# Cross read, GLU and soft mixture of experts on one core: the order of the opening, of batches 0 and 1 and of the end, and TensorE's turns for the states' rows

## The chip, the cores and the metric

The kernel runs on one core of one Trainium2 chip. The metric is the device time of one execution in microseconds (us), the median of three runs. A core has five engines that run side by side, each through its own instructions in program order: TensorE (PE in the profile, its weight loads PEld), VectorE (DVE), ScalarE (ACT), GpSimd (POOL) and SyncE (SP), which here only issues DMA transfers. They wait for each other through semaphores.

## What is computed

8 batches, each with 512 rows and 32 states, 8 heads of 64. Attention in both directions gives 512 + 32 rows of 512 for each batch; all 4608 rows go through a gated linear unit with 1536 inner columns, and its output through a soft mixture of 8 experts with 4 slots each.

```python
scores = scale * x @ state.T;  a = softmax(scores, -1);   xread = a @ state     # 512 rows a batch
scores2 = scale * state @ x.T; a2 = softmax(scores2, -1); sread = a2 @ x        # 32 rows a batch
x = concat(xread, sread)                                   # 4608 rows of 512
xn = x / sqrt(mean(x * x) + 1e-6) * rms_g
h = silu(xn @ w_gate) * (xn @ w_val)                       # 1536 columns
y = h @ w_out
logits = y @ phi                                           # 32 slots
d = softmax(logits, over rows); slot_in = d.T @ y          # 32 slots of 512
for e in range(8): slot_out[e] = relu(slot_in[e] @ w1[e]) @ w2[e]
out = softmax(logits, over slots) @ slot_out
```

## The kernel before

Work goes in nine groups: batches 0 to 7, each 4 tiles of 128 rows, and group 8 (`sread_group`), the 8 x 32 states' rows as 2 tiles. The 1536 inner columns are three chunks `c` of 512. Nothing of y is stored: the read-out of `h` by `w_out` is folded into the logits (`wphi`, that is `w_out @ phi`) and into the slot sums (`slot_h`), which are carried from group to group with a running maximum.

A group and chunk goes like this, each step a short verb in the scripts below. `sw` multiplies a weight chunk with the batch's states on TensorE (8 records; its last argument `r` is the half of the array's rows, 0 or 1), ScalarE copies the product into `wp` (L585), `ss` takes the rounding rest on VectorE (L590). `mg` and `mv` are the gate's and the value's matmul group for one tile, 6 records (12 in group 8), into one of three PSUM buffers of tag `mm`; `sl` is the silu on ScalarE (L624), which frees the gate's buffer; `h` is the product on VectorE (L632), which frees the value's. For the logits, `h` must be turned. In batches 0 and 1 TensorE turns it: `hT` is four 128x128 transposes (L116) and one copy from PSUM (L643, by its last argument on VectorE or ScalarE), and `lg` is then 8 records with 128 rows (`lg_mm128`). In groups 2 to 8 VectorE turns it in 32x32 blocks (`tp`, L660; `tt`, L675, one tile of group 8), and `lg` comes in halves, each 64 matmuls of 32x32 with a weight load for each (`lg_mm`). `p1`, `p2`, `pe`, `p3`, `ps` take the logits through their running softmax; `p1` (L704, L710) copies them out of PSUM, for the 32x32 form half on VectorE, half on ScalarE. `sh` is `slot_h`, the slot sums of one chunk.

Weights arrive as 64-bit words: `wl` loads a piece, `cb` begins it on ScalarE, each `ch` converts half on VectorE (L200, L204, L208) and ends with an add on GpSimd (L212). All of these stand in the opening, two per batch later. `rs` and `ri` are small reciprocals on VectorE. `warm n` are n filler matmuls of 128x128, `br` four, `table` a small exponential that makes ScalarE load its table. `pf` issues one 1 MB load of expert weights, `exp` opens a pool and issues four.

The order of every engine is the order in which the verbs are written: `EARLY` (the opening, batches 0 and 1, the start of 2), `BATCH` (a template for batches 2 to 5, `+0` this batch, `+1` the next), and `LATE` (batches 6, 7 and group 8), run by `follow` under a manual schedule. Behind the scripts stand the last logits' softmax (`post2`, with filler `keep_warm(6)` and `keep_warm(4)`), the slot sums of group 8 and the experts, whose weights come in 12 loads at the end as buffers become free.

Of the kernel before, what the change touches and what calls it, by code (L numbers as in the profile page):

```python
# [20 lines left out]
def kernel(  # L21
# [16 lines left out]
    nc = tc.nc  # L38
# [562 lines left out]
    HH, HT, LGP = {}, {}, {}  # L601
    xsg_t = {}
# [110 lines left out]
    def post2(g):
# [3 lines left out]
        for i in range(2 if g > 1 else 1):  # L717
            for t in range(n):
                o = ps[32 * t : 32 * t + 32, :P]
                if g > 1:  # L720
                    o = o.rearrange("p (b i m) -> p i b m", b=2, i=2)[:, i]
                mm(o, RH[0][:, i, :] if g > 1 else r32, Q[g, "lgs"][t])
# [128 lines left out]
    def wphi_sel():  # L851
# [14 lines left out]
    def wphi_spread(r):  # L866
# [9 lines left out]
        )  # L876

# [174 lines left out]
sw 0 1 1 0; sl 0 1 1; e2 1; warm 1; mg 1 0 3; ss 0 1 1 0; h 1 0 2; sl 1 0 3; ch; mv 1 0 3
sw 0 1 1 1; rs 1; b3 0; ss 0 1 1 1; h 1 0 3; ch; mg 0 1 2; b1 1 0; mg 0 1 3; wl; cb; sl 0 1 2; wl
mv 0 1 0; mv 0 1 1; h 0 1 0; cb; b1 1 1; ch; sl 0 1 3; mv 0 1 2; h 0 1 1; h 0 1 2; ch; mv 0 1 3
sw 0 2 0 0; h 0 1 3; xn 1; sw 0 2 0 1; sw 1 1 0 0; ss 0 2 0 0; ch; ss 1 1 0 0; ss 0 2 0 1; cb; ch
b2 1; sw 1 1 0 1; warm 1; ch; ch; cb; mg 0 2 3; mg 0 2 2; warm 3; sl 0 2 2; sw 0 2 1 0; ss 0 2 1 0
sw 0 2 1 1; mg 0 2 0; wl; sl 0 2 3; ss 0 2 1 1; mg 0 2 1; sl 0 2 0; ss 1 1 0 1; wl; b3 1; mv 0 2 0
h 0 2 0; sl 0 2 1; ch; hT 0 0 0 0; sw 1 1 1 0; mv 0 2 1; hT 0 0 1 0; cb; h 0 2 1; ch; hT 0 0 2 0; ch
cb; mv 0 2 2; mv 0 2 3; ss 1 1 1 0; wp 0 1; wp 0 0; wa 0 0; wa 0 1; warm 2; ch; mg 1 1 0; h 0 2 2
wq 0; sw 1 1 1 1; xt 2; ch; z 2; hT 0 0 3 0; sl 1 1 0; hT 0 1 0 0; mg 1 1 1; wp 1 0; ss 1 1 1 1  # L1060
h 0 2 3; mv 1 1 1; wl; mv 1 1 0; ch; wa 1 0; wl; h 1 1 0; sl 1 1 1; g 2; hT 0 2 0 0; wp 1 1; cb
lg 0 0; ch; a3 2 0; wa 1 1; hT 0 1 1 1; cb; hT 0 1 2 0; a3 2 1; cx 2 0; wq 1; hT 0 1 3 0; ch
mg 1 1 3; cx 2 1; sw 1 2 1 0; tr 2; h 1 1 1; hT 0 2 1 0; hT 1 0 0 0; wp 2 0; ch; tm 2; lg 0 1
mg 1 1 2; wa 2 0; run; ss 1 2 1 0; ts 2; mv 1 1 2; xt 3; sl 1 1 2; sl 1 1 3; ea 2; mv 1 1 3; h 1 1 2
wl; sw 1 2 0 0; hT 0 2 2 0; h 1 1 3; ch; hT 1 0 1 1; hT 0 2 3 1; ss 1 2 0 0; nc 2; sw 1 2 0 1
ss 1 2 0 1; sw 1 2 1 1; ss 1 2 1 1; wp 2 1; wa 2 1; mg 1 2 0; sm 2; wq 2; e2 2; mg 1 2 1; lg 0 2
nm 2 1; p1 0; bt 2; sl 1 2 0; sl 1 2 1; mv 1 2 1; p2 0; bc 2; rs 2; gram 2; pe 0; a3 3 0; bl 2
# [22 lines left out]
h +0 2 3; tp +0 2 1; a3 +2 1; cm +2; lg +0 1 0; tr +2; tm +2; z +2; lg +0 1 1; ts +2  # L1090
# [15 lines left out]
sl 7 0 1; tp 6 2 1; sl 7 0 0; ssum; lg 6 2 0; lg 6 2 1; mv 7 0 1; p1 6; mg 7 0 3; h 7 0 0; ssplit
h 7 0 1; tp 7 0 0; mg 7 0 2; p2 6; ss 7 1 0 1; sl 7 0 3; sl 7 0 2; pf 1; pe 6; mv 7 0 2; ss 7 1 0 0
# [343 lines left out]
```

## Time and profile before

| | us |
|---|---|
| three runs | 645.22, 647.32, 648.64 |
| median | 647.32 |
| the execution that was profiled | 648.35 |
| its span | 646.5 |
| TensorE busy | 615.6 |
| VectorE busy | 457.3 |
| ScalarE busy | 322.6 |
| GpSimd busy | 148.8 |

The profile is of one execution. Its span goes from the first to the last instruction that it records. An engine's busy time is what its instructions cover; a line such as L590 is a line of the kernel. Where an engine stood idle, the profile names what released it, or "issue" where it waited for nothing that the profile shows. The opening with batches 0 and 1 lasts to about 181 us, the four template batches to about 402, and the last main matmul of group 8 ends at 551.39.

### The profile page before, as it was taken

The numbers are of one execution on the slowest core, as the hardware profiler recorded it, in microseconds if no ns is written. First come the engines' busy times: TensorE is split into PE (matmuls) and PEld (weight loads), VectorE is DVE, ScalarE is ACT, GpSimd is POOL, SyncE is SP. The second block draws the span as 40 slices with busy tenths as digits, with TensorE's granted clock in tenths as the row PEclk, the third lists the DMA queues.
The fourth block names the chain that finished last, engine by engine and source line by source line (L and its number), as shares of the span: only waits on it lengthen the run. The fifth ranks groups of instructions, "written<-read, shape, count | busy, mean of one in ns | idle before, by whom it ended". The sixth has DMA issues, their size and how long they took to land.

```text
span 646.5 us, 15895 instructions
## 1 busy us (share of the span) xinstructions
PE 615.6 (95%) x6820; PEld 403.2 (62%) x6820; DVE 457.3 (71%) x902; ACT 322.6 (50%) x506; POOL 148.8 (23%) x183
## 2 busy tenths in 40 slices
PE   5999999999999999999999999999999999899982
PEld 3758666556466676667666675766566768753351
DVE  5988998887958786876877887679476666322152
ACT  4696685567485346346534733851452375100062
POOL 3354444532212021212203211312000000001530
PEclk9999999999999999999999999999999999779997
DMA  8924053530412023022102303200161275949968
GB/s 346 421 99 131 1 196 132 200 133 3 164 52 84 2 99 135 4 87 84 66 2 101 135 2 99 68 1 34 67 257 71 67 261 188 398 162 394 417 228 331
DMA packets 19990, 92.44 MB, mean 143 GB/s; under 512 B 2000, under 2 KB 3408, under 8 KB 12880
## 3 DMA queue, kind: packets, MB, share of 16 engines
q1 hardware_dynamic: 19632, 91.36, 37.5%
q8 instruction: 53, 0.87, 0.6%
q14 instruction: 17, 0.14, 0.1%
q10 hardware_dynamic: 288, 0.07, 0.0%
HBM read 79.37 MB, written 12.06 MB: 141 GB/s over the span
## 4 chain that ended last, share of the span: by engine, by line
PE 80%; DVE 8%; DMA 5%; issue 3%; ACT 3%; SPq 0%; DVEq 0%; ACTq 0%
PE mm L88 47%; PE misc L88 22%; PE lg L88 5%; PE misc L116 3%; DMA ew<-in_w_dram 3%; DVE wp L590 1%; DMA stT<-in_st_t_dram 1%; PE mm L111 1%; DMA out_dram<-ob 1%; DVE wo L208 1%; DVE w L208 1%; DVE w L204 1%; DVE wo L204 0%; DVE h L632 0%; DVE wo L200 0%
## 5 line engine op out<-in xcount | busy, mean ns | idle before, releaser
L88 PE MATMUL mm<-wp,A 128*128 128x512 f32 x1152 | 288.1, 399 | 1.8 <-DVE wp L590 1.4
L88 PEld LDWEIGHTS mm<-wp,A 128*128 128x128 f32 x1152 | 209.6, 188 | 80.1 <-issue 18.0
L585 ACT CAST wp<-misc 128x512 fp32r<-128x512 f32 x96 | 52.8, 590 | 135.5 <-PE misc L88 135.4
L624 ACT ACTIVATE sg<-mm,rinv 128x512 f32<-128x512 f32 x102 | 69.1, 691 | 60.7 <-PE mm L88 40.8
L632 DVE SCALAR_TENSOR_TENSOR h<-mm,rinv,sg 128x512 f32<-128x512 f32 x102 | 75.5, 743 | 26.7 <-PE mm L88 17.8
L590 DVE TENSOR_TENSOR wp<-misc,wp 128x512 fp32r<-128x512 f32 x96 | 63.8, 682 | 13.6 <-ACT wp L585 12.8
L88 PE MATMUL misc<-w,stTg 64*32 64x512 f32 x768 | 64.4, 601 | 0.0
L660 DVE STREAM_TRANSPOSE hT<-h 128x1024 f32<-128x1024 f32 x38 | 46.6, 1235 | 0.3
L88 PE MATMUL lg<-hT,wphi_x 32*32 32x128 f32 (+1 forms) x1344 | 41.4, 264 | 4.0 <-issue 3.8
L88 PEld LDWEIGHTS lg<-hT,wphi_x 32*32 32x32 f32 x1344 | 35.2, 104 | 14.4 <-issue 12.0
L88 PE MATMUL misc<-hT,wphi_x 32*32 32x128 f32 (+1 forms) x1344 | 41.9, 265 | 0.0
L212 POOL TENSOR_TENSOR wo<-wo,raw 128x512 int32<-128x512 int32 x18 | 23.6, 1310 | 70.1 <-ACT sg L624 26.6
L212 POOL TENSOR_TENSOR w<-w,raw 128x512 int32<-128x512 int32 x20 | 26.4, 1322 | 42.3 <-DVE w L208 22.8
L88 PEld LDWEIGHTS misc<-hT,wphi_x 32*32 32x32 f32 x1344 | 34.2, 104 | 2.3 <-issue 2.3
L88 PE MATMUL mm<-wh,xsg 128*128 128x512 f32 x96 | 30.9, 395 | 0.0
L624 ACT ACT_TABLE_LOAD x21 | 26.9, 1283 | 5.6 <-issue 4.7
L88 PE MATMUL misc<-h,ET 128*32 128x512 f32 x204 | 26.3, 599 | 0.8 <-DVE ET L777 0.8
L88 PEld LDWEIGHTS lg<-ident 128*128 128x128 f32 x156 | 20.9, 210 | 6.7 <-issue 5.0
L505 POOL TENSOR_TENSOR A<-aT,A 128x1024 fp32r<-128x1024 f32 x7 | 16.9, 2412 | 33.2 <-ACT A L501 26.9
L88 PE MATMUL lg<-ident 128*128 128x128 f32 x156 | 22.5, 298 | 1.4 <-POOL ident masks.py:199 1.4
L1191 POOL MEMSET sinE<- 128x512 f32 x2 | 1.0, 524 | 96.0 <-PE mm L88 96.0
L88 PEld LDWEIGHTS misc<-w,stTg 64*32 64x32 f32 x768 | 10.8, 105 | 18.6 <-issue 14.7
(246 smaller groups left out, 909.9 us busy)
## 6 DMA issues: line engine op xcount, KB each, us to landing
ew<-in_w_dram SPq DMA_DIRECT2D x25, 1024.0 KB, 7.4
xT<-in_x_t_dram SPq DMA_DIRECT2D x8, 1024.0 KB, 5.4
xn<-in_x_n_dram SPq DMA_DIRECT2D x8, 1024.0 KB, 6.0
ew_w<-in_w_dram SPq DMA_DIRECT2D x7, 1024.0 KB, 9.0
raw<-in_w_val_dram SPq DMA_DIRECT2D x6, 1024.0 KB, 10.5
raw<-in_w_out_dram SPq DMA_DIRECT2D x6, 1024.0 KB, 5.3
raw<-in_w_gate_dram SPq DMA_DIRECT2D x4, 1024.0 KB, 10.5
out_dram<-ob SPq DMA_DIRECT2D x4, 1024.0 KB, 5.9
```

The source lines that it names most:

```text
L88: nc.tensor.matmul(out=o, lhsT=lhsT, rhs=rhs, start=start, stop=stop)
L111: tc.keep_in_program_order(nc.tensor.matmul(out=ps[:, :P], lhsT=ident, rhs=ident, start=True, stop=True))
L116: nc.tensor.transpose(o, i, ident)
L204: nc.vector.tensor_scalar(out=a[:, h], in0=a[:, h], scalar1=3, scalar2=0x3FFFFFF8, op0=ALU.logical_shift_left, op1=ALU.bitwise_and,)
L208: nc.vector.scalar_tensor_tensor(out=a[:, h], in0=hi[:, h], scalar=-0x40000000, in1=a[:, h], op0=ALU.bitwise_and, op1=ALU.bitwise_or,)
L212: nc.gpsimd.tensor_tensor(out=a[:, h], in0=a[:, h], in1=rnd[:, h], op=ALU.add)
L505: nc.gpsimd.tensor_tensor(out=A[:, :, 1, :], in0=T[b, "aT"], in1=A[:, :, 0, :].bitcast(F32), op=ALU.subtract)
L585: nc.scalar.copy(t[:, r, 0, :], ps)
L590: nc.vector.tensor_tensor(out=t[:, r, 1, :], in0=T.pop(("sw", b, c, gv, r)), in1=t[:, r, 0, :].bitcast(F32), op=ALU.subtract,)
L624: nc.scalar.activation(out=sg, in_=ps, func=AF.Silu, scale=RINV[g][:, t : t + 1])
L632: nc.vector.scalar_tensor_tensor(out=HH[g, c][:, t, :], in0=ps, scalar=RINV[g][:, t : t + 1], in1=sg, op0=ALU.mult, op1=ALU.mult,)
L660: nc.vector.transpose(HT[g, c][:, 2 * j : 2 * j + 2, :].rearrange("p t f -> p (t f)"), HH[g, c][:, 2 * j : 2 * j + 2, :].rearrange("p t f ...
```

## The change

Group 8 now takes the form of batches 0 and 1. `by_pe` names the groups that TensorE turns; `lg_mm128`, `logits`, `post1` and `post2` ask it instead of `g < 2`, and take the width of the group, 256 columns. It needs `wphi` in its plain layout to the end, so GpSimd copies it once into the tile of the selector matrices behind `w4 3`.

```diff
+    by_pe = (0, 1, sread_group)
 def lg_mm128(g, c):
-        hT = HT.pop((g, c))
+        hT, n = HT.pop((g, c)), P * gsize(g)
+        w = WPHI4[1] if g > 1 else wphi
-                LGP[g][32 * q : 32 * q + 32, :], wphi[:, 4 * c + q, :], hT[:, q, :],
+                LGP[g][32 * q : 32 * q + 32, :n], w[:, 4 * c + q, :], hT[:, q, :n],
 def logits(g, c, half=1):
-        if g > 1:
+        if g not in by_pe:
 def post1(g):
-        if g < 2:
+        if g in by_pe:
 def post2(g):
-        for i in range(2 if g > 1 else 1):
+        for i in range(1 if g in by_pe else 2):
-                mm(o, RH[0][:, i, :] if g > 1 else r32, Q[g, "lgs"][t])
+                mm(o, r32 if g in by_pe else RH[0][:, i, :], Q[g, "lgs"][t])
 def wphi_spread(r):
+        if r == 3:
+            WPHI4.append(SEL[4])
+            nc.gpsimd.tensor_copy(SEL[4], wphi)
```

All three scripts are written anew. `EARLY` has the same verbs in another order, 82 filler matmuls for 78, and eight of the `hT` copies on VectorE for six. `BATCH` has the same verbs; TensorE's order in it is the same, VectorE's and ScalarE's are not. `LATE` has the same verbs but for group 8: `tp 8`, `tt 8`, the six halves `lg 8 c half` and `br; br` go, six `hT` and three `lg 8 c` come. `exp` stands later, behind `sw 7 2 1 1`. The last lines of `LATE`:

```diff
-table; sl 8 2 1; pf 1; h 8 2 0; tt 8 2 0; h 8 2 1; sh 7 2; pf 1; tt 8 2 1; br; br; lg 8 2 0
-lg 8 2 1; p1 8; pf 1
+mv 8 2 0; h 8 2 0; h 8 2 1; lg 8 1; hT 8 2 0 0; hT 8 2 1 0; sh 7 2; lg 8 2; table; p1 8; pf 1; pf 1
```

TensorE at the end of group 8, before: `hT_6311` and `hT_6440` are the turned chunks 1 and 2, `misc<-h_5822,ET` is `sh 7 2`, `misc<-ident` is `br; br`. The pair of `lg` and `misc` rows stands 16 times for each chunk.

```order
1124 L88 MATMUL lg_6170<-hT_6311,wphi_x_1751 32x64 x2
1125 L88 MATMUL misc<-hT_6311,wphi_x_1751 32x64 x2
1126 L88 MATMUL misc<-h_5822,ET 32x512 x4
1127 L88 MATMUL misc<-ident 128x128 x8
1128 L88 MATMUL lg_6170<-hT_6440,wphi_x_1751 32x64 x2
1129 L88 MATMUL misc<-hT_6440,wphi_x_1751 32x64 x2
```

The same place on TensorE now: L116 with `h_6339` are the turns of chunk 2, `misc<-lgs` is `p2`.

```order
1056 L88 MATMUL mm<-wh_6248,xsg_5421 128x512
1057 L88 MATMUL lg_6179<-hT_6275,wphi_x_1758 32x256 x4
1058 L116 MATMUL misc<-ident,h_6339 128x128 x8
1059 L88 MATMUL misc<-h_5822,ET 32x512 x4
1060 L88 MATMUL lg_6179<-hT_6351,wphi_x_1758 32x256 x4
1061 L88 MATMUL misc<-lgs,r_75 32x128 x2
1062 L111 MATMUL mm<-ident 128x128 x6
```

The 128 small matmuls and the filler behind the last main group are gone, and the turns of chunk 2 stand in front of `sh 7 2`.

TensorE in batch 6, before: the end of chunk 1's logits (`hT_5027`), which here follow the second half of chunk 0's directly; then the `sw` of batch 7 (`misc<-w,stTg`) and main matmuls.

```order
785 L88 MATMUL lg_5117<-hT_5027,wphi_x_1751 32x128 x2
786 L88 MATMUL misc<-hT_5027,wphi_x_1751 32x128 x2
787 L88 MATMUL misc<-w_105,stTg 32x512 x8
788 L88 MATMUL mm<-wp_4973,A_4216 128x512 x6
789 L88 MATMUL mm<-wp_4920,A_4216 128x512 x6
790 L88 MATMUL mm<-wp_4973,A_4216 128x512 x6
791 L88 MATMUL misc<-w_212,stTg 32x512 x8
792 L88 MATMUL mm<-wp_5282,A_4942 128x512 x12
```

The same work now: `hT_4874` is chunk 0, `hT_5037` chunk 1.

```order
745 L88 MATMUL lg_5110<-hT_4874,wphi_x_1758 32x128 x2
746 L88 MATMUL misc<-hT_4874,wphi_x_1758 32x128 x2
747 L88 MATMUL misc<-w_101,stTg 32x512 x8
748 L88 MATMUL mm<-wp_4975,A_4221 128x512 x6
749 L88 MATMUL mm<-wp_4890,A_4221 128x512 x6
750 L88 MATMUL misc<-w_198,stTg 32x512 x8
751 L88 MATMUL lg_5110<-hT_5037,wphi_x_1758 32x128 x2
752 L88 MATMUL misc<-hT_5037,wphi_x_1758 32x128 x2
```

The four `sw` of batch 7 and two main groups moved between the logits of chunk 0 and those of chunk 1.

VectorE in batch 2, around a `ch` (L200, L204, L208), before.

```order
316 L590 TENSOR_TENSOR wp_2100<-misc,wp_2100 128x512
317 L200 TENSOR_SCALAR wo_2094<-wo_2094 128x512
318 L204 TENSOR_SCALAR wo_2094<-wo_2094 128x512
319 L208 SCALAR_TENSOR_TENSOR wo_2094<-raw_2059,wo_2094 128x512
320 L632 SCALAR_TENSOR_TENSOR h_2075<-mm,rinv,sg 128x512
321 L452 TENSOR_TENSOR aT<-misc,aT 128x512
```

And now (L633 is L632 of before).

```order
317 L768 SCALAR_TENSOR_TENSOR sacc<-sacc,al,es 128x1
318 L200 TENSOR_SCALAR wo_2099<-wo_2099 128x512
319 L204 TENSOR_SCALAR wo_2099<-wo_2099 128x512
320 L208 SCALAR_TENSOR_TENSOR wo_2099<-raw_2064,wo_2099 128x512
321 L339 TENSOR_SCALAR rs_2140<-s_1909 128x2
322 L340 RECIPROCAL rs_2140<-rs_2140 128x2
323 L633 SCALAR_TENSOR_TENSOR h_2080<-mm,rinv,sg 128x512
324 L452 TENSOR_TENSOR aT<-misc,aT 128x512
```

`rs` of the next batch moved up to directly behind the first `ch`, ahead of an `h`.

## Rows read from the trace of the kernel before

**Rows 1.** The page: engines' busy time, one DMA queue, the costliest matmul group.

```profile
PE 615.6 (95%) x6820; PEld 403.2 (62%) x6820; DVE 457.3 (71%) x902; ACT 322.6 (50%) x506; POOL 148.8 (23%) x183
...
q8 instruction: 53, 0.87, 0.6%
...
L88 PE MATMUL mm<-wp,A 128*128 128x512 f32 x1152 | 288.1, 399 | 1.8 <-DVE wp L590 1.4
```

**Rows 2.** Windows: stretch and length, busy us by engine, granted clock, DMA share, GB/s.

```profile
20.00:30.00 10.00, 9.06 (x73) 6.34 (x72) 9.67 (x18) 7.40 (x15) 4.33 (x4) 1.00 1.02 420
80.00:100.00 20.00, 19.55 (x185) 12.40 (x177) 18.56 (x36) 15.90 (x21) 8.27 (x7) 1.00 0.42 158
292.00:347.00 55.00, 55.00 (x779) 37.81 (x778) 43.17 (x86) 27.54 (x44) 11.65 (x11) 1.00 0.20 69
```

**Rows 3.** VectorE, 10 to 120 us, by form: busy us, mean ns, idle before.

```profile
L204 DVE TENSOR_SCALAR w<-w 128x512 int32<-128x512 int32 x23 | 15.8, 685 | 0.8
```

**Rows 4.** Timeline of VectorE near 54 us: start, duration, instruction.

```profile
53.45 0.43 DVE L204 TENSOR_SCALAR w<-w 128x512 int32<-128x512 int32 x1
...
54.98 1.40 DVE L204 TENSOR_SCALAR w<-w 128x512 int32<-128x512 int32 x1
```

**Rows 5.** Timeline of TensorE: one `sw` alone, then two side by side.

```profile
105.79 1.06 PE L88 MATMUL misc<-w,stTg 64*32 64x512 f32 x8
...
200.09 1.09 PE L88 MATMUL misc<-w,stTg 64*32 64x512 f32 x16
```

**Rows 6.** Timeline of TensorE in the third half of logits in batch 6.

```profile
452.18 0.27 PE L88 MATMUL lg<-hT,wphi_x 32*32 32x128 f32 x1
454.01 0.29 PE L88 MATMUL lg<-hT,wphi_x 32*32 32x128 f32 x2 [1.56 <-issue]
```

**Rows 7.** Timeline of TensorE at the end of group 8.

```profile
551.39 0.24 PE L88 MATMUL lg<-hT,wphi_x 32*32 32x64 f32 x2
...
552.79 1.06 PE L88 MATMUL misc<-h,ET 128*32 128x512 f32 x8
553.79 2.05 PE L88 MATMUL misc<-ident 128*128 128x128 f32 x16
...
559.08 0.26 PE L88 MATMUL lg<-hT,wphi_x 32*32 32x64 f32 x1 [2.19 <-issue]
...
560.29 0.64 PE L88 MATMUL misc<-lgs,r32h 128*32 128x64 f32 x8 [0.35 <-ACT lgs L710]
```

**Rows 8.** Timeline of VectorE: logits copied out (batch 0), a product of group 8.

```profile
151.75 0.69 DVE L704 COPY lgs<-lg 128x512 f32<-128x512 f32 x1 [1.19 <-PE lg L88]
...
551.56 0.75 DVE L632 SCALAR_TENSOR_TENSOR h<-mm,rinv,sg 128x512 f32<-128x512 f32 x1 [3.99 <-PE mm L88]
```

**Rows 9.** Windows of the end, columns as above.

```profile
560.00:566.00 6.00, 5.71 (x32) 5.32 (x32) 2.17 (x12) 2.31 (x6) 0.52 (x1) 0.51 0.80 326
566.00:573.00 7.00, 6.55 (x30) 4.32 (x29) 3.58 (x11) 0.52 (x2) 0.00 (x0) 0.98 0.49 169
573.00:579.50 6.50, 6.50 (x24) 2.86 (x27) 0.29 (x1) 0.27 (x1) 0.00 (x0) 0.50 0.35 146
583.00:616.00 33.00, 32.19 (x284) 11.48 (x288) 5.53 (x28) 3.15 (x7) 12.07 (x39) 1.00 0.94 385
```

**Rows 10.** The chain that ended last, in order of time: start, length, what.

```profile
566.64 2.77 PE misc L88 x12
...
583.03 7.07 PE mm L88 x64
...
596.59 19.30 DMA ew<-in_w_dram
```

**Rows 11.** Groups by form, 100 to 181 us: TensorE's turns and logits, ScalarE's copies.

```profile
L116 PE MATMUL misc<-ident,h 128*128 128x128 f32 x96 | 13.4, 277 | 0.0
...
L88 PE MATMUL lg<-hT_x,wphi 128*32 128x512 f32 x16 | 2.1, 604 | 0.0
...
L643 ACT COPY hT<-misc 128x512 f32<-128x512 f32 x11 | 6.5, 588 | 3.6 <-PE misc L116 3.4
```

More of the change, by code (lines that the diff above doesn't have):

```diff
@@ L701, in post1 @@
     def post1(g):
-        if g < 2:
-            lgs = k2("lgs")
-            nc.vector.tensor_copy(lgs, LGP.pop(g))
-            Q[g, "lgs"] = [lgs[:, t * P : (t + 1) * P] for t in range(NT)]
+        if g in by_pe:
+            n = P * gsize(g)
+            lgs = k2("lgs")[:, :n]
+            nc.vector.tensor_copy(lgs, LGP.pop(g)[:, :n])
+            Q[g, "lgs"] = [lgs[:, t * P : (t + 1) * P] for t in range(gsize(g))]
             return
@@ L1062 @@
[L1062 to L1067, printed above, removed]
@@ new lines @@
+cb; mg 1 0 3; e2 1; sw 0 1 1 0; h 1 0 2; wl; ch; sl 1 0 3; ss 0 1 1 0; ch; sw 0 1 1 1; mg 0 1 3; cb
+ss 0 1 1 1; mv 1 0 3; warm 5; h 1 0 3; wl; mg 0 1 2; rs 1; hT 0 0 0 0; ch; b1 1 0; mv 0 1 1
+sl 0 1 2; mv 0 1 0; h 0 1 0; sl 0 1 3; b1 1 1; xn 1; cb; ch; mv 0 1 2; h 0 1 1; mv 0 1 3; wl
+h 0 1 2; sw 0 2 0 0; ch; h 0 1 3; ss 0 2 0 0; sw 0 2 0 1; b2 1; sw 1 1 0 0; ch; cb; ss 1 1 0 0
+ss 0 2 0 1; ch; sw 1 1 0 1; warm 3; mg 0 2 3; ch; b3 1; sl 0 2 3; mg 0 2 2; warm 1; sl 0 2 2
+sw 0 2 1 0; ss 0 2 1 0; sw 0 2 1 1; ch; mg 0 2 0; mg 0 2 1; ss 0 2 1 1; mv 0 2 1; wl; sl 0 2 0; ch
@@ new lines @@
+mv 0 2 0; h 0 2 0; sw 1 1 1 0; ss 1 1 0 1; sl 0 2 1; ch; hT 0 0 1 0; wl; hT 0 2 0 1; cb; h 0 2 1; ch
+mv 0 2 2; mv 0 2 3; hT 0 0 2 0; ss 1 1 1 0; hT 0 0 3 1; cb; warm 1; wp 0 0; wp 0 1; warm 4; ch; xt 2
+mg 1 1 0; g 2; h 0 2 2; wl; sl 1 1 0; sw 1 1 1 1; h 0 2 3; wa 0 0; ch; wp 1 0; wa 0 1; ss 1 1 1 1
+hT 0 1 0 0; mg 1 1 1; mv 1 1 0; ch; wl; wq 0; a3 2 0; cx 2 0; lg 0 0; h 1 1 0; mv 1 1 1; sl 1 1 1
+wa 1 0; cb; z 2; wp 1 1; hT 0 2 1 0; ch; wa 1 1; hT 0 1 1 0; hT 0 1 2 1; cb; a3 2 1; wq 1; run; ch
@@ new lines @@
+mg 7 1 1; p3 6; h 7 0 2; sw 7 1 1 0; sh 6 0; pf 1; sw 7 1 1 1; h 7 0 3; sl 7 1 1; ss 7 1 1 0
+ss 7 1 1 1; tp 7 0 1; sw 7 2 0 0; mg 7 1 0; mv 7 1 0; mv 7 1 1; ps 6; sl 7 1 0; mg 7 1 2; h 7 1 0
+lg 7 0 0; lg 7 0 1; sw 7 2 0 1; h 7 1 1; mg 7 1 3; mv 7 1 2; sl 7 1 2; ss 7 2 0 1; ss 7 2 0 0
+h 7 1 2; mv 7 1 3; sl 7 1 3; h 7 1 3; tp 7 1 0; sh 6 1; sw 7 2 1 0; sw 7 2 1 1; exp; mg 7 2 0
+sl 7 2 0; mg 7 2 1; ss 7 2 1 0; sl 7 2 1; ss 7 2 1 1; mv 7 2 1; mv 7 2 0; tp 7 1 1; h 7 2 0; h 7 2 1
+mg 7 2 2; mv 7 2 2; mg 7 2 3; sl 7 2 2; lg 7 1 0; h 7 2 2; sl 7 2 3; lg 7 1 1; cn 5; ws 0 0 0
@@ new lines @@
+ws 0 0 1; ws 0 0 2; ws 0 0 3; mv 7 2 3; mg 8 0 0; tp 7 2 0; h 7 2 3; tp 7 2 1; pf 1; sh 6 2; pf 1
+mg 8 0 1; lg 7 2 0; ws 1 0 0; ws 1 0 1; lg 7 2 1; pf 1; ws 1 0 2; ws 1 0 3; p1 7; mv 8 0 0; ws 0 1 0
+sl 8 0 1; p2 7; mv 8 0 1; ws 0 1 1; ws 0 1 2; sl 8 0 0; h 8 0 0; pe 7; p3 7; ws 0 1 3; sh 7 0
+h 8 0 1; mg 8 1 1; hT 8 0 0 1; ce 6; hT 8 0 1 0; mg 8 1 0; pf 1; lg 8 0; sl 8 1 1; ws 1 1 0; pf 1
+ws 1 1 1; pf 1; sh 7 1; sl 8 1 0; ws 1 1 2; ws 1 1 3; ws 0 2 0; mv 8 1 0; ws 0 2 1; h 8 1 0
+mv 8 1 1; ws 0 2 2; ws 0 2 3; pf 1; h 8 1 1; ws 1 2 0; ps 7; mg 8 2 1; ws 1 2 1; ws 1 2 2
```

119 lines of the change are left out of this document (52 added, 67 removed).

## The prediction

> **What bounds the kernel now.** I read the page's shares first. TensorE is busy 615.6 of the span's 646.5 us [rows 1], so time comes off only where TensorE works less, waits less, or runs faster. Then I read stretches, because the share is a mean over stages. In the opening VectorE is the fuller engine: 9.67 us of 10 at 20 to 30 us, 18.56 of 20 at 80 to 100, while TensorE's share there includes filler matmuls [rows 2]. In the middle, TensorE is busy 55.00 us of 55.00 and VectorE 43.17 [rows 2]: there only fewer TensorE cycles or a new wait can change the time. Then the operations of the opening's VectorE by kind [rows 3] and a pair of them one by one [rows 4], the price of the read-out matmuls alone and in pairs [rows 5], the one idle time of TensorE in the late batches [rows 6], the end on TensorE [rows 7] and VectorE [rows 8], the granted clock there [rows 9], and the chain that ended last [rows 10]. The prices of the form that replaces the turns stand in batches 0 and 1, which have it already [rows 11].
>
> The execution shown took 648.35 us (its span 646.5 and 1.85 around it); the median of the runs is 647.32, 1.03 lower. Sums go against 648.35 and are lowered by 1.03 at the end.
>
> **The opening and batches 0 and 1** have the same verbs in another order, four filler matmuls more, two of the copies of turned rows moved from ScalarE to VectorE. Two things have a price.
>
> First, pairs. Each `sw` is 8 records. Alone it holds TensorE 1.06 us; two that stand side by side and use opposite row halves (last argument 0 and 1) take 1.09 together [rows 5]. A new pair so saves 2 x 1.06 - 1.09 = 1.03 us. The scripts of the opening have 5 such pairs before and 9 now. Of the four, one takes the place of a triple with an `a3` between, which the trace already overlaps, and one new neighbour of an `a3` makes up for that. Two of the four lie before 110 us, where VectorE is the fuller engine, two behind it, where TensorE is. I count the later two in full, -2.1, and the earlier two as hidden.
>
> Second, VectorE. A conversion step `ch` is three VectorE operations and then one add on GpSimd (L212). The middle one, L204, takes 0.43 us, and 1.40 where it starts while that add of the step before still runs [rows 4]. That is why its mean is 685 ns over 23 [rows 3]: 23 x (0.685 - 0.43) = 5.9 us, six events of about 0.97. Steps directly behind a step: 8 in the opening before, 6 now. The change also takes the `ri` chain from behind a step. That is -3 x 0.97 = -2.9 us of VectorE; two copies more cost 2 x 0.69 [rows 8], so -1.5. Two small operations now stand behind a step that did not before, up to +1.9 back. I let half of -1.5 reach TensorE and round: -0.9. Every other VectorE and TensorE operation is as before, and weight and row loads only change places among themselves in SyncE's queue, where the DMA engines are full (1.02 at 20 to 30 us [rows 2]), so which arrives first changes, not when all have. **Opening: -3.0**, with bounds -5.6 (all four pairs and all of the VectorE gain: 4.1 + 1.5) and +1.5 (three new waits of half a microsecond, no gain).
>
> **The four middle batches** keep TensorE's order; only VectorE and ScalarE change. Two moves could reach TensorE. `rs` (two operations on 128 x 2) now stands directly behind a `ch`, four times, ahead of an `h`. By [rows 4] it can be held 0.97 us, and the `h` behind it, that frees a PSUM buffer. And the silu of tile 3 (`sl` 0 3) moves behind two more matmul groups: its buffer, one of three, stays taken, so the groups between live on two. Each such group is 6 matmuls of 399 ns, which overlap (288.1 us busy over 1152, so 0.25 each [rows 1]): 1.5 us, in which one `h` of 0.75 [rows 8] has to free a buffer; the margin is some tenths. VectorE has 55.0 - 43.2 = 11.8 us spare per batch [rows 2]. I take **+0.5** for all four, bounds 0 and +2.4.
>
> **Late batches.** Three halves of 32x32 logits follow each other before (`lg` 6 0 1, 6 1 0, 6 1 1), 192 matmul records and as many weight loads, and in the third TensorE stands idle 1.56 us, put down to "issue": no semaphore, nothing that the profile shows is awaited [rows 6]. A queue of kind "instruction" moved 53 packets [rows 1], 0.87 MB, so code does come in by DMA; that the idle time is code that came late is my reading, not a row's. Now four `sw` and matmul groups stand between, at most two halves in a row, which elsewhere run without such a gap. **-1.6**, bounds -1.6 and 0. One more pair of `sw` in batch 6: **-1.0**, bounds -1.0 and 0 [rows 5].
>
> **The end.** Call T the end of the last main matmul group (551.39 before, where the logits follow it [rows 7]). Ahead of T now stand two 128-row logits less one half pair: the four turns of tiles `hT` 8 0 and 8 1, 96 records that took 13.4 us for 24 turns, so 0.56 each and some 0.5 with their overlap [rows 11], that is +2.0; one `lg` of 256 columns, half of the 2.1 us / 2 that 512 columns cost [rows 11], +0.55; taken away two 32x32 halves, 552.79 - 551.39 = -1.4 [rows 7]. T comes **1.1 later** (bounds +0.6, +1.5).
>
> Behind T before: logits 1.40, `sh` 1.0, two `br` 2.0, logits until the copies, with a second idle of 2.19 "issue" within them; the first matmul of `p2` starts at 560.29, 8.90 behind T [rows 7]. Now: `lg` 8 1 0.55; the first turn at about T + 1.0, when `h` 8 2 0 is there; `h` 8 2 1 follows at T + 1.65 (each 0.75, the first from T + 0.17 before [rows 8]), its turn ends at T + 2.25; `sh` 7 2 1.06 [rows 7] hides the ScalarE copy of 0.59 [rows 11]; `lg` 8 2 0.55, T + 3.85; one VectorE copy of half of 512 columns, 0.69 at most [rows 8]. `p2` starts near T + 4.4: **-4.5** (bounds -5.0, -3.0). The copy goes to VectorE alone, behind two `h` and an `acc`, which are through by then.
>
> [...] What the row shows: one 32x32 half takes 0.70 us [rows 7]. [...]
>
> Between `p2` and `slot_h` lie 566.64 - 560.29 = 6.35 us [rows 7, 10], of which the granted clock was 0.51 with TensorE busy 5.71 of 6 [rows 9], the lower of its two levels. At the upper one up to half of 5.7 us comes back, -2.8. Before the fall stood the 2.19 us of idle time, which now goes. But the clock fell again at 573 with TensorE busy 6.50 of 6.50 [rows 9], so I can't say from rows that it holds: **-1.6**, between 0 and -2.8.
>
> **What is late next.** From 583.03 the expert matmuls run, then TensorE waits 19.30 us for expert weights [rows 10] with DMA at 0.94 [rows 9]. These loads are freed by those matmuls, so they start earlier by as much as the chain does, if the loads ahead are done: DMA was busy 0.49 of 7.0 and 0.35 of 6.5 us before [rows 9], so 3.6 + 4.2 = 7.8 us are spare and the end's net -5.0 passes.
>
> Sum: 648.35 - 3.0 + 0.5 - 1.6 - 1.0 + 1.1 - 4.5 - 1.6 = 638.25; at the median 637.2.
>
> **Rivals.**
> - *Only the end's order pays.* The opening gives nothing and the clock falls as before: 637.2 + 3.0 + 1.6 = 641.8. For it: VectorE at 9.67 of 10, whose work is the same. Chance 0.20.
> - *The change doesn't remove the code stalls, only moves them*: 1.6 + 2.2 come back at other long runs of small matmuls: 641.0. For it: nothing in a row says why just these two places; against: other pairs of halves run through. Chance 0.13.
> - *Loads become late*: the four loads of `exp` are issued some 25 us later and the end is shorter, so each expert load beyond the 7.8 us spare adds its own 2.7 us (1.05 MB at 385 GB/s [rows 9]); with the whole net gain of 5.0 eaten 642.2. Chance 0.07.
> - *Slower*: in the middle batches the two-buffer stretch makes TensorE wait some 0.7 us for the silu of tile 2, and the granted clock falls behind it for as long as at 573, 6.5 us at 0.50 [rows 9], so half of them lost: 0.7 + 3.25 = 3.95 per batch, 15.8 in four, 637.2 - 0.5 + 15.8 = 652.5. It decides from 3.5 us per batch on ((650.6 - 636.7) / 4). Against: after 1.56 us idle at 452 [rows 6] the clock stayed at 1.00. Chance 0.06.
>
> **How the numbers follow.** Forecast 0.54, its own range 633.5 to 641. The low end 632: every bound (-5.6, 0, -1.6, -1.0, +0.6, -5.0, -2.8) gives 632.95, less 1.03. The high end takes in the second to fourth case and half of what they add up to together: 643.5; beyond lie the slow case and mixes. Within 0.5% (3.2 us, about what a measurement can tell from no change) means 644.1 to 650.6: two or three rivals at once, to which I give 0.12 of what the cases above hold. Slower 0.07 with one such mix; the rest, 0.81, is faster.
>
> **What would show it.** VectorE's L204 mean in the opening near 640 ns and less filler needed; no idle "issue" over 1 us around the logits of batch 6; `p2` 4 to 5 us behind the last main group; clock 1.00 until the expert stage; the wait for expert weights of the same length, but earlier. Wrong if `hT` 8 waits for its copies, if the middle batches grow, or if the opening ends no earlier than now.

## The result, and the profile after

The changed kernel takes 639.89 us, the median of four runs (639.03 to 641.11), against 646.64 for the kernel before in its four runs; the ratio is 0.9895, 95% interval 0.9862 to 0.9927. Forecast were 637.2, between 632.0 and 643.5. So the time lies in the range and on the forecast side, 2.7 us short of the sum.

The execution that was profiled took 641.11, the highest of the four, with a span of 639.3; its fellow before took 648.35 and 646.5. Laid side by side, the two traces fall into seven stretches:

| stretch | before, us | after, us | difference | forecast |
|---|---|---|---|---|
| to the first main matmul of batch 2 | 181.23 | 182.62 | +1.39 | -3.0 |
| three template batches (2 to 4) | 164.62 | 164.14 | -0.48 | +0.5 |
| the fourth, batches 6, 7 and group 8, to T | 205.54 | 203.61 | -1.93 | -1.6 - 1.0 + 1.1 = -1.5 |
| T to the first matmul of `p2` | 8.90 | 4.56 | -4.34 | -4.5 |
| `p2` to the slot sums of group 8 | 6.35 | 3.70 | -2.65 | -1.6 |
| slot sums to the experts | 16.39 | 17.69 | +1.30 | 0 |
| experts to the end of the span | 63.47 | 62.98 | -0.49 | 0 |
| sum | 646.50 | 639.30 | -7.20 | -10.1 |

Two stretches come out worse than forecast by more than a microsecond: the opening, by 4.4 us, and the one behind the slot sums, by 1.3. Two come out about 1.0 better: the template batches, and `p2` to the slot sums.

The page of after: engines' busy time and the instruction queue, as in [rows 1].

```profile
PE 608.6 (95%) x6472; PEld 397.8 (62%) x6472; DVE 453.7 (71%) x902; ACT 317.7 (50%) x503; POOL 148.8 (23%) x184
...
q8 instruction: 51, 0.84, 0.5%
```

TensorE has 348 records fewer and 7.0 us less busy time. In the end the timeline of TensorE (start, duration, instruction, idle before and its releaser) answers [rows 7]:

```profile
550.36 0.64 PE L88 MATMUL lg<-hT,wphi_x 128*32 128x256 f32 x8
551.35 1.38 PE L116 MATMUL misc<-ident,h 128*128 128x128 f32 x8 [0.35 <-DVE h L633]
552.65 1.06 PE L88 MATMUL misc<-h,ET 128*32 128x512 f32 x8
553.54 0.61 PE L88 MATMUL lg<-hT,wphi_x 128*32 128x256 f32 x8
554.92 0.41 PE L88 MATMUL misc<-lgs,r 128*32 128x128 f32 x4 [0.77 <-DVE lgs L707]
```

Logits, turns, `sh 7 2`, logits, `p2`: the forecast had the steps at T, T + 1.0, T + 2.25, T + 3.3 and T + 4.4; they stand at T, + 0.99, + 2.29, + 3.18 and + 4.56. No "issue" stands among them. The copy `lgs` on VectorE waited for an `acc` (L801) of 0.75, which the forecast had taken to be through by then; that is the 0.77 in the last row.

The windows of after (busy us of PE, PEld, DVE, ACT, POOL, granted clock, DMA share, GB/s) show the two stretches that came out worse, beside [rows 2] and [rows 9]:

```profile
21.50:28.40 6.90, 6.90 (x39) 3.12 (x38) 5.91 (x10) 3.81 (x6) 3.97 (x4) 0.51 1.00 413
...
560.00:564.20 4.20, 4.20 (x21) 3.06 (x15) 1.88 (x3) 0.27 (x1) 0.00 (x0) 1.00 0.99 410
564.20:574.50 10.30, 10.30 (x39) 4.21 (x38) 0.40 (x2) 0.27 (x1) 0.04 (x1) 0.50 0.67 265
...
576.30:609.30 33.00, 32.98 (x288) 11.56 (x288) 5.52 (x28) 3.15 (x7) 11.75 (x39) 1.00 0.91 378
```

The granted clock fell to 0.51 in the opening, where it had stayed at 1.00 before; and between the last main group and the experts it fell once, at 564.2, to 0.50 for 10.2 us, where it had fallen twice, at 559 and 573, for 6.8 us each [rows 9].

In the expert stretch the forecast had taken the 19.30 us of [rows 10] for a wait of TensorE. They are a transfer that stands in the chain; TensorE was busy 32.19 of 33.00 us meanwhile [rows 9], and idle for 0.79 us at the transfer's end. TensorE in the kernel before:

```profile
615.93 1.06 PE L88 MATMUL so<-ew,hz 128*32 128x512 f32 x8 [0.79 <-DMA ew<-in_w_dram]
```

Now it is busy 32.98 of 33.00 us, and the transfer is gone from the chain (DMA holds 1% of it, 5% before). The stretch is only 0.49 shorter: loads and matmuls are near a tie there.

### The profile page after: what moved, and what is told of

It is laid out like the page before. It is cut to its first block, busy times and chain, and to the rows that moved or that the text cites. A ratio compares the mean times of both kernels' runs of the same rounds, so it can differ in the third digit from the quotient of the medians.

```text
span 639.3 us, 15210 instructions
## 1 busy us (share of the span) xinstructions
PE 608.6 (95%) x6472; PEld 397.8 (62%) x6472; DVE 453.7 (71%) x902; ACT 317.7 (50%) x503; POOL 148.8 (23%) x184
## 4 chain that ended last, share of the span: by engine, by line
PE 85%; DVE 4%; ACT 2%; DMA 1%; issue 1%; SPq 0%; DVEq 0%; ACTq 0%
PE mm L88 49%; PE misc L88 23%; PE lg L88 6%; PE misc L116 4%; PE so L88 2%; DMA stT<-in_st_t_dram 1%; DMA out_dram<-ob 1%; DVE wp L590 1%; DVE w L204 1%; DVE w L208 1%; DVE h L633 1%; PE mm L111 0%; ACT ob L1330 0%; DVE w L200 0%; ACT L625 0%
## 5 line engine op out<-in xcount | busy, mean ns | idle before, releaser
L633 DVE SCALAR_TENSOR_TENSOR h<-mm,rinv,sg 128x512 f32<-128x512 f32 x102 | 75.2, 744 | 26.4 <-PE mm L88 23.8
L88 PE MATMUL misc<-w,stTg 64*32 64x512 f32 x768 | 62.7, 611 | 0.4 <-issue 0.4
L662 DVE STREAM_TRANSPOSE hT<-h 128x1024 f32<-128x1024 f32 x36 | 44.1, 1235 | 0.4
L212 POOL TENSOR_TENSOR wo<-wo,raw 128x512 int32<-128x512 int32 x18 | 23.5, 1306 | 76.6 <-DVE wo L208 40.7
L88 PEld LDWEIGHTS lg<-hT,wphi_x 32*32 32x32 f32 (+1 forms) x1176 | 31.6, 104 | 12.0 <-issue 10.4
L88 PE MATMUL lg<-hT,wphi_x 32*32 32x128 f32 (+1 forms) x1176 | 38.0, 272 | 0.0
L212 POOL TENSOR_TENSOR w<-w,raw 128x512 int32<-128x512 int32 x20 | 26.6, 1331 | 43.6 <-DVE w L208 17.4
L88 PE MATMUL misc<-hT,wphi_x 32*32 32x128 f32 x1152 | 36.5, 270 | 0.0
L88 PEld LDWEIGHTS misc<-hT,wphi_x 32*32 32x32 f32 x1152 | 30.2, 103 | 0.0
L505 POOL TENSOR_TENSOR A<-aT,A 128x1024 fp32r<-128x1024 f32 x7 | 16.9, 2412 | 45.3 <-ACT A L501 34.7
L88 PE MATMUL misc<-xT,stT 64*32 64x512 f32 x128 | 17.5, 679 | 9.2 <-DMA stT<-in_st_t_dram 9.2
L193 ACT ACTIVATE raw<-raw 128x1024 int32<-128x1024 uint32 x19 | 22.0, 1159 | 0.0
```

The costliest lines, as they stand in the source:

```text
L88: nc.tensor.matmul(out=o, lhsT=lhsT, rhs=rhs, start=start, stop=stop)
L193: nc.scalar.activation(out=rnd, in_=lo.bitcast(U32), func=AF.Copy, scale=2.0 ** -29)
L212: nc.gpsimd.tensor_tensor(out=a[:, h], in0=a[:, h], in1=rnd[:, h], op=ALU.add)
L505: nc.gpsimd.tensor_tensor(out=A[:, :, 1, :], in0=T[b, "aT"], in1=A[:, :, 0, :].bitcast(F32), op=ALU.subtract)
L633: nc.vector.scalar_tensor_tensor(out=HH[g, c][:, t, :], in0=ps, scalar=RINV[g][:, t : t + 1], in1=sg, op0=ALU.mult, op1=ALU.mult,)
L662: nc.vector.transpose(HT[g, c][:, 2 * j : 2 * j + 2, :].rearrange("p t f -> p (t f)"), HH[g, c][:, 2 * j : 2 * j + 2, :].rearrange("p t f ...
```

## The experiments

### The opening alone undone

```diff
 changed kernel
-    EARLY of after
+    EARLY of before
```

> The changed kernel with the opening's order of before. Theory A (the new opening costs some 1.4 us: in its trace the middle batches start at 182.6 instead of 181.2, and the clock is at its lower level from 21.6 to 28.4 us): the middle batches start near 181.2 again, the clock is 1.00 from 20 to 30 us, and the time is about 1.4 us under the changed kernel's, near 638.5. Rival B (the prediction: the new opening saves some 3 us, and one trace only shows it badly): 2 to 3 us above the changed kernel's, near 642.5.

Measured: 638.89 us (638.38 to 639.78, five runs), 0.9885 of before (0.9864 to 0.9905), so 1.0 below the changed kernel. The middle batches start at 181.62 and the clock is 1.00 from 20 to 30 us. By the medians, and by the two traces, the new opening thus costs about a microsecond as it stands, though the runs of the two kernels overlap (the changed kernel's lie from 639.03 to 641.11). Theory A holds, with two thirds of its size; rival B, the prediction, falls.

### The end alone

```diff
 kernel before, its three orders kept, with the change's code (by_pe)
-tp 8 0 0; ... lg 8 0 0; lg 8 0 1; ... tp 8 1 0; ... lg 8 1 0; lg 8 1 1
+hT 8 0 0 1; ... hT 8 0 1 0; ... lg 8 0; ... hT 8 1 0 1; hT 8 1 1 0; ... lg 8 1
-h 8 2 0; tt 8 2 0; h 8 2 1; sh 7 2; pf 1; tt 8 2 1; br; br; lg 8 2 0; lg 8 2 1; p1 8; pf 1
+h 8 2 0; hT 8 2 0 0; h 8 2 1; hT 8 2 1 0; sh 7 2; pf 1; lg 8 2; p1 8; pf 1
```

> The kernel of before with all three orders of before, only group 8 turned by TensorE and taken in the 128-row form, without the two fillers br. Theory A (the gain is the end's, and no order is needed for it): the last main matmul group ends about 1 us later, the last logits' softmax starts 4 to 5 us behind it instead of 8.9, the slot sums 3.7 us behind that instead of 6.35, the idle time of 1.56 in batch 6 stays; 5 to 6 us under before, 641 to 642. Rival B (the clock holds there only through the new order of the late batches): the clock falls to its lower level before the slot sums as before, these start 6 us behind the softmax, and the gain is 3 us, near 644.

Measured: 642.98 us, 0.9948 of before (0.9931 to 0.9964), -3.5. In the trace T comes 1.15 later within its stretch (206.69 for 205.54 us; forecast +1.1), `p2` 4.50 behind T, the slot sums 3.96 behind `p2`, the idle time in batch 6 is 1.38. The stretches are those of theory A and the clock held without the new order, so rival B falls. The total is 1 us short of A. Both the expectation and the forecast were summed against a trace that was 1.8 us above the median; a second trace of before, below, shows part of the reason.

### Three halves of logits in a row

```diff
-lg 6 0 1; sw 7 0 0 0; sw 7 0 0 1; ...; sw 7 0 1 0; sw 7 0 1 1; lg 6 1 0; ce 5; lg 6 1 1
+lg 6 0 1; lg 6 1 0; lg 6 1 1; sw 7 0 0 0; sw 7 0 0 1; ...; sw 7 0 1 0; sw 7 0 1 1; ce 5
```

> The changed kernel, with the four sw of batch 7 and two main matmul groups of batch 6 put behind the logits of chunk 1 of batch 6, so that three halves of 32x32 logits follow each other as before. Theory A (three halves in a row use up the code faster than it comes): an idle time of 1 to 2 us put down to issue stands in the third half again, and the stretch grows by that. Rival B (only the place in the program counts, where a piece of code ended by chance): no idle time over 0.5 us in it, and the time as the changed kernel's.

TensorE in the third half, in this kernel, in the one with the end alone, and in the kernel before run once more:

```profile
450.83 0.30 PE L88 MATMUL lg<-hT,wphi_x 32*32 32x128 f32 x2 [0.92 <-issue]
```

```profile
454.74 0.29 PE L88 MATMUL lg<-hT,wphi_x 32*32 32x128 f32 x2 [1.38 <-issue]
```

```profile
454.46 0.29 PE L88 MATMUL lg<-hT,wphi_x 32*32 32x128 f32 x2 [1.39 <-issue]
```

All four traces with three halves in a row have the idle time (0.92, 1.38, 1.39, 1.56 [rows 6]); none of the eight without has any over 0.25 us there. The stretch from the fourth template batch to T is 204.38, against 203.61 in the changed kernel's trace and 202.64 to 203.44 in the seven others without the row. The one execution took 639.57 us, which lies among the changed kernel's runs, so the time by itself shows nothing. The row of halves makes the idle time, theory A, and it is worth 0.9 to 1.6 us. That it is code that comes late stays a reading of "issue". The rows nearest to it: in after the instruction queue moved 51 packets, 0.84 MB, so about 16 KB each, and three halves are 192 matmuls and 192 weight loads. Whether a packet came late in the third half no run here shows. The opening, the same as the changed kernel's, kept the clock at 1.00 in this execution, and the middle batches start at 181.00.

### Filler where the opening stood idle

```diff
-nm 0 1; warm 5; ch; cb; table; bp 0 0
+nm 0 1; warm 12; ch; cb; table; bp 0 0
```

> The changed kernel with 7 more filler matmuls (14 records) ahead of the first turn of a in the opening, where TensorE stands idle for 2.04 us before the clock falls at 21.6 us. Theory A (the clock falls behind that idle time and this is what the new opening loses): clock 1.00 from 20 to 30 us, the middle batches start 1 to 1.5 us earlier, time near 638.6. Rival B (VectorE sets the opening's end, so the clock there costs nothing): clock 1.00, the middle batches start within 0.4 us of the changed kernel's, same time. Rival C: the clock falls all the same.

Before the clock fell, TensorE in after had this row, with 2.04 us of idle time; the window behind it is from this experiment:

```profile
20.21 1.06 PE L116 MATMUL misc<-ident,a 128*128 128x128 f32 x8 [2.04 <-DVE a L356]
```

```profile
20.00:30.00 10.00, 9.22 (x88) 6.14 (x87) 9.72 (x18) 7.28 (x15) 4.32 (x4) 1.00 1.03 422
```

Measured: 637.86 us (637.50 to 638.21, five runs), 0.9866 of before (0.9847 to 0.9886): 2.0 below the changed kernel, with no overlap of the runs. The clock is 1.00, the middle batches start at 181.11, 1.51 earlier. Theory A fits the time. Of the cause it shows less: the same opening without these fillers kept the clock in the experiment above, where the idle time in that place was 0.82, and one run further down had the filler and a fall at 26 us all the same. So that the idle time is the cause of the fall is open. Open too is whether the fall is the whole difference of 2.0. The trace puts it at 1.5, but of the changed kernel's four runs the one with the highest mean clock, 0.987, took 640.00 us, more than each of the five with the filler (0.984 to 0.986); and the three traces with a mean of 0.987 or 0.988 have no fall in the opening.

With the filler, the new opening is 1.03 below the old one (637.86 for 638.89), with no overlap of the runs: a third of the forecast 3.0. The traces show half of that. The middle batches start at 181.23 to 181.68 in the four with the old opening, and at 180.79 to 181.11 in the four that have the new order unaltered and a held clock (one of them without the filler).

### The kernel before, once more

No edit.

> The kernel of before, unchanged, for a second trace. The end alone gave 3.5 us by the medians but 6.1 by the stages of the two traces. Theory A (the idle times put down to issue, 1.56 us in batch 6 and 2.19 in the last logits, change from execution to execution, and the first trace had long ones): one of them is shorter here by a microsecond or more, and the time nearer 646.5. Rival B (they are the same in each): both within 0.3 us of the first trace, and the slot sums again start 15 us behind the last main group.

Measured: 647.09, span 645.3. The idle time in batch 6 is 1.39 (1.56 in the first trace), the one in the last logits 1.47 (2.19):

```profile
558.81 0.21 PE L88 MATMUL lg<-hT,wphi_x 32*32 32x64 f32 x1 [1.47 <-issue]
```

T to `p2` takes 7.94 instead of 8.90, `p2` to the slot sums 5.41 instead of 6.35. So both idle times stand in each of the two traces, but the second is 0.7 us shorter and the first 0.2; the clock, lower for only 3.4 us there, gave back another 0.9. But from the slot sums to the experts this trace takes 17.75 us for 16.39, with one lower stretch of the clock of 10.2 us, as in after. The experts start at 582.94 and 583.03 all the same. Neither theory holds as worded: one idle time is shorter, as theory A said, but by 0.7 us where it asked for one. The first trace had the larger idle times, and so promised 1.9 us more than an execution like this one had to give, in the two stretches behind T.

### The early pairs taken apart

```diff
-ch; sw 0 1 1 1; mg 0 1 3; cb
+ch; mg 0 1 3; sw 0 1 1 1; cb
-ch; sw 1 1 0 1; warm 3; mg 0 2 3; ch
+ch; warm 3; mg 0 2 3; sw 1 1 0 1; ch
```

> The opening with the fillers of the run before, its two new pairs of sw ahead of 110 us taken apart by a main matmul group between (0 1 1 and 1 1 0). Theory A (VectorE sets the opening to there, the pairs only made room for filler and waits): TensorE's sw take 1.9 us more, the middle batches start within 0.4 us of 181.1. Rival B (TensorE sets it): 1.5 to 2 us later, near 183.

TensorE from 10 to 110 us, groups of instructions (busy us, mean ns, idle before and releasers), with the pairs and with them apart:

```profile
L88 PE MATMUL mm<-wp,A 128*128 128x512 f32 x185 | 47.2, 402 | 1.5 <-DVE wp L590 0.9 <-DVE h L633 0.4 <-ACT sg L625 0.2
...
L88 PE MATMUL misc<-w,stTg 64*32 64x512 f32 x152 | 14.6, 601 | 0.0
```

```profile
L88 PE MATMUL mm<-wp,A 128*128 128x512 f32 x183 | 47.0, 402 | 1.9 <-DVE wp L590 1.5 <-DVE h L633 0.4
...
L88 PE MATMUL misc<-w,stTg 64*32 64x512 f32 x152 | 15.2, 601 | 0.0
```

The middle batches start at 181.77, 0.66 later, and this execution's first matmul stood 0.32 earlier than its fellow's, so the price is about 1.0: half of what rival B said, and not the nothing of theory A. The one execution took 639.09 us. The `sw` take 0.6 us more, not 1.9. The first pair goes from 1.09 to 2.12; the second, 1 1 0, had cost 1.87 though it stood side by side, so its halves hardly overlapped; and the next pair behind them, which was not touched, comes down from 1.68 to 1.09. The wait of TensorE for VectorE's `wp` at 97 us grew from 0.29 to 1.10, since it came there earlier and VectorE at nearly the same time (96.55 and 96.81). So VectorE sets the pace there. The forecast had counted neither pair; one paid in part, and one hardly overlapped.

### The late pair taken apart

```diff
-sw 1 2 1 1; sw 1 2 0 0; wa 2 0; ss 1 2 1 0; ts 2; mg 1 1 2
+sw 1 2 1 1; wa 2 0; ss 1 2 1 0; ts 2; mg 1 1 2; sw 1 2 0 0
```

> The same opening with the new pair of sw at about 140 us taken apart by a main matmul group (1 2 1 1 and 1 2 0 0). Theory A (TensorE sets the time there, so a pair is worth what it saves): the middle batches start 0.9 us later than 181.1. Rival B (the pair is hidden there too, behind the waits around the running softmax of batch 0): within 0.3 us.

TensorE at the next `sw` and `a3`, with the pair in front of it and with the pair apart:

```profile
143.94 1.06 PE L88 MATMUL misc<-w,stTg 64*32 64x512 f32 x8
145.07 1.06 PE L88 MATMUL misc<-xT,stT 64*32 64x512 f32 x8
146.07 0.62 PE L88 MATMUL misc<-wo,phis 128*32 128x512 f32 x2
```

```profile
145.10 0.63 PE L88 MATMUL misc<-w,stTg 64*32 64x512 f32 x4
145.22 0.63 PE L88 MATMUL misc<-xT,stT 64*32 64x512 f32 x4
145.55 0.61 PE L88 MATMUL misc<-w,stTg 64*32 64x512 f32 x4
145.65 0.63 PE L88 MATMUL misc<-xT,stT 64*32 64x512 f32 x4
146.22 0.62 PE L88 MATMUL misc<-wo,phis 128*32 128x512 f32 x2
```

The one execution took 638.06 us. The middle batches start at 181.24, 0.13 later, as rival B said, but for another reason than its own. Taken apart, the pair costs 1.16 us by 145.10. Then the `sw` and the `a3` behind it overlap, 1.12 us for both, where with the pair they stood one behind the other, 2.13. In both the `a3` starts at 145.1 to 145.2. It reads batch 3's transposed rows `xT` and states, whose transfer is issued at 140.0, when a buffer comes free, and whose rows land at 144.8, the states at 144.9. In after, TensorE's row at that place names it:

```profile
146.62 1.06 PE L88 MATMUL misc<-xT,stT 64*32 64x512 f32 x8 [0.16 <-DMA stT<-in_st_t_dram]
```

So the transfer sets this place, and of the two new neighbourhoods, the pair and the `a3`, only one can pay.

### The last logits copied by ScalarE

```diff
-            nc.vector.tensor_copy(lgs, LGP.pop(g)[:, :n])
+            (nc.vector.tensor_copy if g < 2 else nc.scalar.copy)(lgs, LGP.pop(g)[:, :n])
```

> The changed kernel with the opening's fillers, and the last logits copied out of PSUM by ScalarE instead of VectorE, where the copy waits for the slot sums' acc (0.75 us). Theory: the softmax starts 0.3 to 0.5 us earlier behind the last main group (4.0 to 4.2 instead of 4.50), the rest as it was, 637.5. Rival: ScalarE has the exponential's table load in front of the copy, and nothing is gained or 0.5 us lost.

ScalarE there:

```profile
551.04 1.28 ACT L998 ACT_TABLE_LOAD   x1
552.34 0.20 ACT L998 ACTIVATE dummy<-ones 128x1 f32<-128x1 f32 x1
552.45 0.35 ACT L707 COPY lgs<-lg 128x256 f32<-128x256 f32 x1
```

T to `p2` grew from 4.56 to 4.81, and the time is 638.49 (638.17 to 638.69), 0.6 above its fellow with the copy on VectorE. The rival holds: `table` stands in front of the copy.

### The `a3` behind its rows

```diff
-sw 1 2 0 1; a3 3 0; ss 1 2 0 1; wp 2 1; wa 2 1; e2 2; sm 2; mg 1 2 0; wq 2; mg 1 2 1
+wp 2 1; sw 1 2 0 1; a3 3 0; wa 2 1; ss 1 2 0 1; e2 2; sm 2; wq 2; mg 1 2 0; mg 1 2 1
```

> The opening with the fillers; at 144 us the order sw 1 2 0 1, a3 3 0, wp 2 1, main group, wq 2 becomes wp 2 1, sw 1 2 0 1, a3 3 0, wq 2, main group. Theory A (the a3 cannot start before the rows of batch 3 land at 144.8 us, and so doesn't overlap the sw in front of it, 1.14 and 0.99 us instead of 0.45 and 0.67 as in the run with the late pair taken apart): both overlap now, the middle batches start 0.8 to 1.0 us earlier, at 180.2, and the time is near 637.0. Rival B (the main group then waits for the sw's rounding rest on VectorE): the gain is given back there, start within 0.3 us of 181.1.

Measured: 637.08 us, six runs from 636.33 to 639.62, 0.9852 of before (0.9822 to 0.9881), the lowest median of all, though its runs overlap those with the filler alone (637.50 to 638.21). The execution that was profiled is the 639.62: its clock fell at 26 us for 3.4 us and in the end for 10.2. By `mg 1 1 0` it is 0.8 us behind the kernel with the filler (116.51 for 115.69), at `lg 0 2` it is level (151.26 for 151.24), so the new order gave 0.8 us back in between, as theory A said; the middle batches start at 181.07. In this trace the `sw` and `a3` took 1.56 together, not 1.12.

### The middle batches' template of before

```diff
 the kernel with the filler
-    BATCH of after
+    BATCH of before
```

> The opening with the fillers, the middle batches' template of before. Theory A (VectorE's and ScalarE's new order there moves nothing on TensorE): the four batches take 164.1 to 165.1 us as in all runs so far, with the scatter coming from idle times put down to issue; time 637.9. Rival B (the rs behind a ch and the two-buffer stretch cost): 0.5 to 2 us less.

Measured: 637.42 us (637.07 to 638.65), the stretch of the first three template batches 164.15 us beside 164.13. No difference: theory A. Over all twelve traces the stretch takes 163.9 to 165.8; the 165.79 has idle times put down to "issue", 0.78 in one place.

## Why the prediction was right, and where its sum was off

**The opening, -3.0: the step that failed.** It gave +1.0 by the medians as it stands and -1.0 with the filler. In the first trace it ended 1.39 later, which the prediction had named as a sign that it is wrong. Three of its parts went wrong.

The two pairs behind 110 us were counted in full, -2.1, because TensorE is the fuller engine there (before, from 110 to 181 us, it is busy 71.10 us and VectorE 60.08). TensorE's `sw` did become cheaper there (8.64 us before, 7.49 after), but the two neighbourhoods stand 6 us apart and the second of them, the `a3`, can't start before its rows land. The forecast said that the loads "only change places", and took the transfer that is issued when a matmul frees a buffer for no term. Share of busy time was read as the limit, though one wait that ends last on a transfer decides.

The VectorE term read rows right and counted the wrong thing. Up to 120 us L204 was long, 1.40 to 1.45 us, six times before, and it is so six times after. On `w` its mean came down from 685 [rows 3] to 653, on `wo` it rose from 427. Before, L208 and L200 on `w` had 693 and 464 ns. After:

```profile
L204 DVE TENSOR_SCALAR w<-w 128x512 int32<-128x512 int32 x23 | 15.0, 653 | 0.8
L208 DVE SCALAR_TENSOR_TENSOR w<-raw,w 128x512 int32<-128x512 int32 x20 | 14.8, 742 | 0.7
...
L200 DVE TENSOR_SCALAR w<-w 128x512 f32<-128x512 f32 x22 | 10.9, 497 | 0.0
...
L204 DVE TENSOR_SCALAR wo<-wo 128x512 int32<-128x512 int32 x7 | 4.0, 567 | 0.2
```

All three operations on `w` and `wo` together took 56.2 us of VectorE from 10 to 120 us before and 55.3 after, with one L208 (0.7) fewer in the window: of the 1.9 us forecast for the steps, 0.2 came. What counts is whether GpSimd is at work when a VectorE operation of this kind starts, in whatever step, not which step stands in front. Over all twelve traces L204 takes 1.39 to 1.46 us in each of the 75 cases in which it starts beside an L212 (13 of them in before and after), and 0.41 to 0.43 in the 489 in which GpSimd is idle (80 of them). GpSimd's other operations lengthen it as well (0.71 us beside L482). The `ri` chain, that the change took from directly behind a step, was still held for 1.24 us (1.29 before; row below), since only one short operation stands between.

The clock was a rival only in the middle batches. In the opening it had stood at 1.00 [rows 2], and the sum had no term for it; it cost 1.5 us in the one trace of after that has it.

**The middle batches, +0.5: 0.** The `rs` behind a `ch` was not held, nor was the `h` behind it. VectorE and GpSimd in batch 2 after:

```profile
214.38 0.17 DVE L340 RECIPROCAL rs<-rs 128x2 f32<-128x2 f32 x1
```

```profile
214.40 1.31 POOL L212 TENSOR_TENSOR wo<-wo,raw 128x512 int32<-128x512 int32 x1 [6.37 <-ACT sg L625]
```

The first operation of `rs`, L339, had run (162 ns on average) before the add started, and the second, L340, started 0.02 us before it. For L340 the order does not matter: over the twelve traces it takes 0.17 us also in the eight cases in which it starts beside such an add. Nor is the `h` held, 0.74 to 0.75 us in 153 cases. L339 can be: 0.30 to 0.32 us in eight, 0.16 otherwise in after. So it is the kind of the operation as well as the order that decides, and of the three only L339 could have been held; it came first. In [rows 4] likewise it is the second operation behind a step that is long: the first is already running. The `ri` chain of the opening met the add after its start. VectorE and GpSimd there, after:

```profile
32.08 1.24 DVE L556 TENSOR_SCALAR ri<-rv 128x4 int32<-128x4 int32 x1
```

```profile
31.98 1.31 POOL L212 TENSOR_TENSOR w<-w,raw 128x512 int32<-128x512 int32 x1 [3.25 <-DVE ncm L257]
```

The operation that came second lasts 1.24 us, where L556 takes 0.17 in the eight other cases of after, in which GpSimd is idle; it ends at 33.32, the add at 33.29. What holds it no row shows. The two-buffer stretch cost nothing: 164.15 us with the old template, 164.13 with the new.

**Late batches, -2.6.** From the fourth template batch to T the kernel with the old opening needs 202.64, the one with the end alone 206.69: -4.05. The idle time is 1.38 of it, `sw` 1.22 (19.21 to 17.99 over 32), and the other main groups 0.8 (72 of them, 1.447 to 1.436 start to start), which had no term: a main group that stands alone takes 1.53 us with the end alone, one in a row of three 1.43, and 28 rows of them stand where 31 stood. The remaining 0.65 is not broken down.

**T later, +1.1:** +1.15. **T to `p2`, -4.5:** -4.34 against the first trace, -3.38 against the second. **Clock behind `p2`, -1.6:** -2.65 in the trace, and the clock held there in every one of the ten kernels with the new form. About 0.3 of it is not the clock's: the end alone, with the clock held as well, takes 3.96 us there, the changed kernel 3.70. But the forecast stopped there: behind the slot sums the clock fell again in all of them, for about 6.8 or 10.2 us, and with 10.2 that stretch takes 17.7 us instead of 16.4 to 16.9. Some of the end's gain is so given back in some executions. The 7.8 us of spare DMA time were right for this: the stretch of the experts did not grow.

Of the rivals, "only the end's order pays", 641.8, is nearest by its mechanism: the opening gave nothing. The 639.89 is below it because the clock did hold up to the slot sums and the late batches gave more. The idle times put down to "issue" did not move elsewhere: the largest in after is 0.38 us behind 60 us. The late loads did not come, nor the slow case. Of the signs, `p2` and the idle time in batch 6 came as said; the clock at 1.00 until the experts and a wait for weights of the same length did not.

That the total lies in the range is in part luck: in the table above the opening and the stretch behind the slot sums come out 5.7 us worse than the sum had them, and the other stretches together 2.8 better.

By medians: end alone -3.5, the new order of the late batches (and of the middle ones, which is nothing) -4.1, the new opening +1.0; together -6.6.

## What to carry to other kernels

A saving on the fuller engine of a stretch is only worth what the next wait leaves of it: look in the trace for the transfer or the copy that ends last at that place, and count two savings that wait for the same one once. Replacing a long run of tiny matmuls behind the last large one by a few wide ones paid in latency (8.90 to 4.56 us from T to `p2`), not in TensorE's time: behind T it was busy 6.36 us before and 3.35 after, but 2.05 of the difference was filler, and T came 1.15 later. Before adding up terms against one trace, set that execution beside the median: stalls that differ between executions count only with their mean. A transfer in the chain that ended last is not yet an idle time of the engine behind it: look at the engine's own row.

## What the runs showed that was not expected

- In the same opening the granted clock fell at 21.6 us for 6.8 us in one execution and stayed at 1.00 in another (182.62 and 181.00 to the middle batches); with more filler it fell in one of six traces (at 26 us, 3.4 us long).
- Behind the slot sums the clock fell for about 6.8 or for 10.2 us, in the row of after with TensorE busy 10.30 of 10.30; which of the two comes was not settled, and is worth 1.3 us.
- Three halves of 64 small matmuls in a row met an idle time each time (0.92 to 1.56 us), two in a row at that place none over 0.25; two in a row as the last logits, with DMA at 1.01, met 1.47 and 2.19.
